# Column halves for the last output tile, and joined stores in the last chunk, of an attention and gated feed-forward kernel

## The chip, the cores and the metric

The kernel runs on one core of a Trainium2 chip. Its time is the device time of one execution in microseconds (us). The engines are called as the profile calls them: PE does the matmuls (PEld its weight loads), DVE, ACT and POOL do elementwise work, SP only issues transfers. Transfers run on 16 DMA engines; SP and ACT both issue them here, each into a queue of its own.

## What is computed

```python
# attention: q, k, v are (8, 8, 576, 64)
q_d = q.reshape(B, H, Sd, 4, D).mean(axis=3)          # and k_d, v_d
out_d = softmax(scale * q_d @ k_d.T) @ v_d
out_up = np.repeat(out_d, 4, axis=2)
mask = np.abs(pos[:, None] - pos[None, :]) < 4
out_local = softmax(where(mask, scale * q @ k.T, -1e9)) @ v
x = (out_up + out_local).transpose(0, 2, 1, 3).reshape(4608, 512)
# feed-forward
h = x @ w_in                                           # 512 -> 2048
g = h * np.clip(h + 3.0, 0.0, 6.0) / 6.0
out = g @ w_out                                        # 2048 -> 512, float32
```

The output is 4608 rows of 512 floats, so a row has 2048 bytes.

## The kernel before

The 4608 tokens are worked in nine chunks of 512. For each chunk the attention result is split into a high and a low part, multiplied by w_in, gated, split again and multiplied by w_out; each product is three matmuls (high by high, high by low, low by high). The last two chunks are planned together by `plan_pair`, which forms their first product in another way; their second product is ordinary again, in `gemm2` (L1392).

Every piece of work is an `op` of the class `Plan`, with an engine (or a choice), a cost, what it waits for and what it frees. `emit` (L1765) plays the plan through by these numbers and so decides the order in which the instructions are written out, engine by engine. The waits between engines are set afterwards by the framework, on semaphores. For transfers there are eight semaphores, called DMAHW0 to DMAHW7, taken in turn: a transfer waits until the one eight before it, on the same semaphore, has landed.

In the last chunk, the sums of the four output tiles (128 tokens by 512 columns each, m = 0 to 3) grow in four PSUM banks, o0 to o3. The last two blocks of w_out (`together`, L1402) are done tile by tile: six matmuls of 512 columns for tile 0, then for tile 1, 2 and 3 (L1420 to L1422). So the tiles become final one after the other. `plan_store` (L992) takes each of them out of PSUM with the factor 1/6: tiles 0 and 2 on ACT (L1013), 1 and 3 on DVE (L1015). It then stores the tile.

A tile can't be stored in one plain transfer. The output in DRAM is laid out so that 36 consecutive tokens of a batch entry lie 32 rows apart, and the next 36 tokens begin one row further. `stores` (L977) cuts a tile where such a group ends and yields the pieces (first partition, rows, place in DRAM); `put` (L988) issues one transfer for a piece. In the last chunk the pieces of a tile are sorted by size and dealt out in turn to SP and to ACT (L1023 to L1026). SP and ACT each do what stands in their queue in order, so an ACT eviction stands behind the stores ahead of it.

Of the kernel before, what the change touches and what calls it, by code (L numbers as in the profile page):

```python
# [13 lines left out]
AF = mybir.ActivationFunctionType  # L14
ALU = mybir.AluOpType
# [3 lines left out]
DM, DFF = 512, 2048  # L19
# [37 lines left out]
def tile_local_down_attention_moe(ctx, tc, q_all, k_all, v_all, _qk_loc, _v_loc, w_in, w_out, ident_d, _mask_d, out):  # L57
# [916 lines left out]
    otile, st_o, gemms = {}, {}, []  # L974
    n0 = len(PART) - 2

    def stores(t, cnt):  # L977

        p = 0
        while p < cnt:  # L980
            b, s = divmod(t + p, S)
            c, r = divmod(s, RP)
            k = min(RP - r, cnt - p)
            bp, b2 = divmod(b, NB2)
            yield p, k, (bp * NI * P + r * 32 + b2 * NC + c) * DM
            p += k

    def put(eng, ob, p, k, first):  # L988
        eng.dma_start(
            bass.AP(tensor=out.tensor, offset=out.offset + first, ap=[[32 * DM, k], [1, DM]]), ob[p:p + k])  # L990

    def plan_store(n, m, ready, frees):  # L992

        at = PART[n][0] + m * P
        ok = "ob" if n < n0 else "ob7"

        def ev(eng):
            st_o[n, m] = ob = buf(ok, (n, m), [P, DM])
            if eng is nc.scalar:
                eng.activation(ob, otile[n, m], AF.Copy, scale=1.0 / 6.0)  # L1000
            else:
                eng.tensor_scalar(ob, otile[n, m], 1.0 / 6.0, None, op0=ALU.mult)

        def store():
            for piece in stores(at, P):
                put(nc.sync, st_o[n, m], *piece)

        if n == len(PART) - 1:

            def ev_last(eng):  # L1010
                st_o[n, m] = buf("obz", (n, m), [P, DM])
                if eng is nc.scalar:
                    eng.activation(st_o[n, m], otile[n, m], AF.Copy, scale=1.0 / 6.0)  # L1013
                else:
                    eng.tensor_scalar(st_o[n, m], otile[n, m], 1.0 / 6.0, None, op0=ALU.mult)  # L1015

            def store_half(mine, eng):
                for piece in mine:
                    put(eng, st_o[n, m], *piece)

            e = [op("ACT" if m % 2 == 0 else "DVE", (0.60, 0.69)[m % 2], partial(ev_last, nc.scalar if m % 2 == 0 else nc.vector), [ready],
                    take=[("obz", (n, m))], free=[frees])]
            every = sorted(stores(at, P), key=lambda x: -x[1])  # L1023
            for eng, on_, mine in (("SP", nc.sync, every[0::2]), ("ACT", nc.scalar, every[1::2])):
                op(eng, 0.5 * len(mine), partial(store_half, mine, on_), e, free=[("obz", (n, m))],
                   size=dma(sum(k for _, k, _ in mine), 2048), nd=len(mine))  # L1026
            return
        e = op(on("ob", 1.0), 0, ev, [ready], take=[(ok, (n, m))], free=[frees], dl=start_of(n + 1) + TF * LAG)
        op("SP", 2.0, store, [e], free=[(ok, (n, m))], size=dma(P, 2048), dl=start_of(n + 1) + 10, nd=len(list(stores(at, P))))

    second = {}
# [1 line left out]
    def plan_moe(n):  # L1033
# [89 lines left out]
            plan.free_after(("gh" + k0, ("gh", key)), ops_)  # L1123
            plan.free_after(("gl" + k0, ("gl", key)), ops_)
        for m in range(nm):
            plan_store(n, m, ops_[m], (f"o{m}", n))
        return [last1]


# [10 lines left out]
    def plan_pair(prev_last, keeps):  # L1140
# [233 lines left out]
        for c in range(2):  # L1374
            n = n0 + c
            for i, f in enumerate(order):
                key = n, f

                def hi(eng, key=key):
                    parts7["h", key] = buf("ghb", ("gh", key), [P, TOK])  # L1380
                    copy_on(eng, parts7["h", key], gz[key])

                def lo(eng, key=key):
                    parts7["l", key] = buf("glb", ("gl", key), [P, TOK])
                    eng.tensor_tensor(parts7["l", key], gz[key], parts7["h", key].bitcast(F32), op=ALU.subtract)

                hold = [units_[-2][5], units_[-1][5]] if c or i > 1 else []
                d = op(on("ghi", TOK), 0, hi, [gz_ready[key]] + hold, take=[("ghb", ("gh", key))], lock=True)
                e = op(on("gl", TOK), 0, lo, [d], take=[("glb", ("gl", key))], free=[place_of(ORDER7.index(f // 2), key)], lock=True)
                parts7["ready", key] = [d, e]  # L1390

            def gemm2(m, f, n=n, c=c):  # L1392
                if f == order[0]:
                    otile[n, m] = bank(f"oe{m}" if c == 0 else f"o{m}", n)
                ms = slice(m * P, (m + 1) * P)
                gh, gl = parts7["h", (n, f)], parts7["l", (n, f)]
                for i, (gt, wt) in enumerate(((gh, 0), (gh, 1), (gl, 0))):
                    nc.tensor.matmul(  # L1398
                        otile[n, m], gt[:, ms], wout[f][:, wt],
                        start=(f == order[0] and i == 0), stop=(f == order[-1] and i == 2))  # L1400

            together = order[-2:] if c else order[-1:]  # L1402
            for i, f in enumerate(order):
                dl = base + len(ORDER7) * UNIT7 + (NF * c + i) * UNIT7 * 2 / 7
                after = parts7["ready", (n, f)] + [w_done["o", f]] + back.get(f, [])
                if f in together:
                    continue
                if i == 0:
                    ops_ = []
                    for m in range(4):  # L1410
                        ops_.append(op("PE", 0.683, partial(gemm2, m, f), after + prev[-1:], take=[(f"oe{m}" if c == 0 else f"o{m}", n)], dl=dl, rec=3))
                        prev.append(ops_[-1])
                else:
                    ops_ = [op("PE", 2.73, lambda f=f, g=gemm2: [g(m, f) for m in range(4)], after + prev[-1:], dl=dl, rec=12)]
                    prev += ops_
                for k in ("gh", "gl"):
                    plan.free_after((k + "b", (k, (n, f))), ops_)
            ops_ = []
            after = [x for f in together for x in parts7["ready", (n, f)] + [w_done["o", f]] + back.get(f, [])]
            for m in range(4):  # L1420
                ops_.append(op("PE", 0.683 * len(together), lambda m=m, g=gemm2, fs=together: [g(m, f) for f in fs], after + prev[-1:], dl=dl, rec=3 * len(together)))
                prev.append(ops_[-1])  # L1422
            for f in together:
                for k in ("gh", "gl"):
                    plan.free_after((k + "b", (k, (n, f))), ops_)
            for m in range(4):
                plan_store(n, m, ops_[m], (f"oe{m}" if c == 0 else f"o{m}", n))


    def busy(n):  # L1430
# [613 lines left out]
```

## Time and profile before

| | us |
|---|---|
| median of 3 runs (907.33 to 909.1) | 908.95 |
| the profiled execution, its own time | 907.05 |
| its span, first to last instruction | 905.3 |
| PE busy in the span | 885.7 (98%) |
| DVE, ACT, POOL busy | 631.4, 406.7, 224.8 |

The span is what the trace shows. The profiled execution took 1.75 us more than its span, and lies 1.9 us under the median of the timed runs.

### The profile page before, as it was taken

What the parts mean: (1) busy time and instruction counts of PE and PEld (TensorE: products, weight loads), DVE (VectorE), ACT (ScalarE), POOL (GpSimd) and SP (SyncE); (2) the same over time, 40 slices, a digit from 0 to 9 for tenths busy, and PEclk for the clock granted to TensorE, in tenths of its full rate; (3) what the DMA queues carried; (4) which work ended last, traced back from release to release, by engine and by line L of the source; (5) the groups of instructions that cost most, each with busy time, mean ns of one, the idle gap of its engine ahead of it and who ended that gap; (6) DMA issues with size and microseconds to landing.
All of it is one profiled execution on the core that took longest, in us unless ns stands there. A gap on an engine that the chain in (4) does not pass through costs nothing.

```text
span 905.3 us, 19616 instructions
## 1 busy us (share of the span) xinstructions
PE 885.7 (98%) x7044; PEld 720.5 (80%) x7044; DVE 631.4 (70%) x1174; ACT 406.7 (45%) x1404; POOL 224.8 (25%) x293
## 2 busy tenths in 40 slices
PE   8889999999999999999999999999999999999997
PEld 5667877887888888888888778888787888888886
DVE  6888987677836778676765785767666799964330
ACT  5786844656414446443432444335544344332100
POOL 2735554241301121211111210114222133400000
PEclk9999999999999999999999999999999999999999
DMA  9898667667624474754463656677665102222011
GB/s 217 222 272 272 168 145 133 131 126 141 131 71 89 95 148 99 144 101 97 99 137 72 120 113 164 151 183 185 170 140 117 23 24 70 76 88 104 31 29 47
DMA packets 325809, 111.94 MB, mean 124 GB/s; under 512 B 258640, under 2 KB 306640, under 8 KB 325712
## 3 DMA queue, kind: packets, MB, share of 16 engines
q1 hardware_dynamic: 325110, 109.92, 51.9%
q8 instruction: 56, 0.92, 0.4%
q10 hardware_dynamic: 602, 0.77, 0.3%
q14 instruction: 41, 0.34, 0.1%
HBM read 79.58 MB, written 31.05 MB: 122 GB/s over the span
## 4 chain that ended last, share of the span: by engine, by line
PE 84%; DMA 5%; SPq 5%; DVE 3%; issue 1%; ACT 1%; POOL 0%; DVEq 0%
PE o L1100 30%; PE h L1050 29%; PE o L1398 5%; PE o L1283 4%; PE h L1398 2%; PE a L1283 2%; PE a L1398 2%; SPq L373 2%; PE h L1283 2%; PE a L718 2%; PE h L761 1%; DMA arena<-in_v_dram 1%; DMA rows<-in_q_dram 1%; DMA early<-in_v_dram 1%; PE a L523 1%
## 5 line engine op out<-in xcount | busy, mean ns | idle before, releaser
L1050 PE MATMUL h<-rounded,wp 128*128 128x512 f32 x1344 | 318.3, 393 | 7.3 <-DVE arena L1060 5.0
L1100 PE MATMUL o<-wp,rounded 128*128 128x512 f32 x1344 | 323.1, 393 | 0.1
L1050 PEld LDWEIGHTS h<-rounded,wp 128*128 128x128 f32 x1344 | 252.1, 189 | 63.9 <-DVE arena L1060 7.2
L1100 PEld LDWEIGHTS o<-wp,rounded 128*128 128x128 f32 x1344 | 249.7, 188 | 53.5 <-DVE wp L211 0.5
L1056 ACT ACTIVATE arena<-h 128x512 f32<-128x512 f32 x112 | 66.3, 592 | 125.2 <-PE h L1050 116.1
L1060 DVE SCALAR_TENSOR_TENSOR arena<-arena,h 128x512 f32<-128x512 f32 x112 | 75.8, 677 | 50.9 <-ACT arena L1056 50.1
L573 ACT ACTIVATE arena<-arena 128x64 f32<-128x64 f32 x240 | 80.1, 336 | 0.5
L1068 DVE TENSOR_TENSOR rounded<-arena,rounded 128x512 fp32r<-128x512 f32 x83 | 58.8, 709 | 28.0 <-PE o L1100 24.8
L121 DVE CAST rounded<-arena 128x512 fp32r<-128x512 f32 (+1 forms) x93 | 43.0, 466 | 33.9 <-PE o L1100 17.4
L1068 POOL TENSOR_TENSOR rounded<-arena,rounded 128x512 fp32r<-128x512 f32 x29 | 39.4, 1358 | 97.4 <-PE o L1100 51.8
L379 DVE STREAM_TRANSPOSE arena<-arena 128x576 f32<-128x576 f32 x56 | 43.2, 774 | 28.2 <-DMA arena<-in_k_dram 14.2
L119 ACT CAST rounded<-arena 128x512 fp32r<-128x512 f32 (+6 forms) x57 | 36.9, 653 | 48.4 <-DVE arena L1060 19.8
L590 POOL TENSOR_TENSOR arena<-arena 128x640 f32<-128x640 f32 (+1 forms) x24 | 28.3, 1177 | 106.0 <-DVE arena L583 73.5
L454 POOL TENSOR_TENSOR arena<-arena 96x256 f32<-96x256 f32 (+1 forms) x23 | 18.4, 802 | 144.5 <-DMA arena<-in_v_dram 106.9
L452 DVE TENSOR_REDUCE arena<-arena 128x128 f32<-128x512 f32 (+1 forms) x31 | 33.2, 1075 | 19.8 <-DMA arena<-in_v_dram 10.3
L573 ACT ACTIVATION_READ_ACCUMULATOR arena<-arena 128x1 f32 x240 | 45.4, 189 | 0.0
L1398 PE MATMUL o<-wp,rounded 128*128 128x512 f32 x192 | 43.7, 389 | 0.0
L693 ACT ACTIVATE arena<-h 128x144 f32<-128x144 f32 x24 | 7.0, 290 | 79.1 <-PE h L677 79.1
L1398 PEld LDWEIGHTS o<-wp,rounded 128*128 128x128 f32 x192 | 36.1, 188 | 7.5
L549 ACT ACTIVATE arena<-arena 128x1 f32<-128x1 f32 (+1 forms) x78 | 15.1, 194 | 49.7 <-DVE arena L562 49.6
L411 DVE TENSOR_REDUCE arena<-arena 128x144 f32<-128x576 f32 x45 | 33.1, 742 | 1.9 <-PE h L523 1.6
L455 POOL TENSOR_TENSOR arena<-arena 96x128 f32<-96x128 f32 (+1 forms) x23 | 10.9, 474 | 88.7 <-PE h L677 81.1
(258 smaller groups left out, 1227.7 us busy)
## 6 DMA issues: line engine op xcount, KB each, us to landing
arena<-in_v_dram SPq DMA_DIRECT2D x58, 160.0 KB
pl<-arena SPq DMA_DIRECT2D x26, 320.0 KB
arena<-pl SPq DMA_DIRECT2D x104, 80.0 KB
rawp<-in_w_in_dram SPq DMA_DIRECT2D x16, 512.0 KB
rawp<-in_w_out_dram SPq DMA_DIRECT2D x16, 512.0 KB
arena<-in_q_dram SPq DMA_DIRECT2D x112, 72.0 KB
arena<-in_k_dram SPq DMA_DIRECT2D x112, 72.0 KB
arena<-in_v_dram SPq DMA_DIRECT2D x28, 256.0 KB
```

The lines of the kernel that those rows point to most:

```text
L119: nc.scalar.copy(out_, in_)
L121: eng.tensor_copy(out_, in_)
L379: nc.vector.transpose(out=qk[kind], in_=qk[kind])
L452: eng.tensor_reduce(out=vd, in_=raw.rearrange("p r e -> p e r"), op=ALU.add, axis=AX.X)
L573: nc.scalar.activation(x[:, j], x[:, j], AF.Exp, bias=m[:, j:j + 1], scale=0.125, accum_out=s[:, j:j + 1])
L1050: nc.tensor.matmul(st["ps"], win[f][:, wt, kk * P:(kk + 1) * P], xs[part][:, kk], start=(kk == 0 and i == 0), stop=(kk == NK - 1 and i == ...
L1056: nc.scalar.activation(st["t"], st["ps"], AF.Relu, bias=3.0)
L1060: nc.vector.scalar_tensor_tensor(out=t, in0=t, scalar=6.0, in1=st["ps"], op0=ALU.min, op1=ALU.mult)
L1068: eng.tensor_tensor(st["gl"], st["t"], st["gh"].bitcast(F32), op=ALU.subtract)
L1100: nc.tensor.matmul(otile[n, m], gt[:, ms], wout[f][:, wt], start=(f == 0 and i == 0), stop=(f == NF - 1 and i == 2),)
L1283: nc.tensor.matmul(ps[which], stationary(w, wt, kb), xs[x, kb][:, part], start=first and kb == 0 and q == 0, stop=last and kb == 1 and q = ...
L1398: nc.tensor.matmul(otile[n, m], gt[:, ms], wout[f][:, wt], start=(f == order[0] and i == 0), stop=(f == order[-1] and i == 2))
```

## The change

Three things are changed, all for the last chunk alone.

First, the six matmuls of the last tile (m = 3) become twelve of 256 columns: six for the left half, then six for the right half, in the same bank. Second, each half of that tile is taken out and stored on its own: the left half on DVE, the right half on ACT. Third, `stores` joins whole groups of 36 rows that follow one another, and `put` writes them as one transfer with three dimensions: groups, rows of a group, columns.

```diff
-    def stores(t, cnt):
+    def stores(t, cnt, joined=False):
         ...
             k = min(RP - r, cnt - p)
+            while joined and r == 0 and k % RP == 0 and k + RP <= min(cnt - p, S - s):
+                k += RP
         ...
-    def put(eng, ob, p, k, first):
+    def put(eng, ob, p, k, first, cs=slice(0, DM)):
+        width = cs.stop - cs.start
+        to = [[32 * DM, k]] if k <= RP else [[DM, k // RP], [32 * DM, RP]]
         eng.dma_start(
-            bass.AP(tensor=out.tensor, offset=out.offset + first, ap=[[32 * DM, k], [1, DM]]), ob[p:p + k])
+            bass.AP(tensor=out.tensor, offset=out.offset + first + cs.start, ap=to + [[1, width]]), ob[p:p + k, cs])
         ...
-            every = sorted(stores(at, P), key=lambda x: -x[1])
-            for eng, on_, mine in (("SP", nc.sync, every[0::2]), ("ACT", nc.scalar, every[1::2])):
-                op(eng, 0.5 * len(mine), partial(store_half, mine, on_), e, free=[("obz", (n, m))],
-                   size=dma(sum(k for _, k, _ in mine), 2048), nd=len(mine))
+            every = sorted(stores(at, P, True), key=lambda x: -x[1])
+            for h in range(halves):
+                cs = slice(h * DM // halves, (h + 1) * DM // halves)
+                name, eng = on_[(m + h) % 2]
+                e = op(name, (0.60, 0.69)[(m + h) % 2] / halves + 0.04 * (halves - 1), partial(ev_last, eng, cs), ready[h:h + 1] if halves > 1 else ready,
+                       take=[("obz", (n, m))], free=[frees])
+                for name, eng, mine in (("SP", nc.sync, every[0::2]), ("ACT", nc.scalar, every[1::2])):
+                    if mine:
+                        op(name, 0.5 * len(mine), partial(store_half, mine, eng, cs), [e], free=[("obz", (n, m))],
+                           size=dma(sum(k for _, k, _ in mine), 2048 // halves), nd=len(mine))
         ...
                 for i, (gt, wt) in enumerate(((gh, 0), (gh, 1), (gl, 0))):
                     nc.tensor.matmul(
-                        otile[n, m], gt[:, ms], wout[f][:, wt],
-                        start=(f == order[0] and i == 0), stop=(f == order[-1] and i == 2))
+                        otile[n, m][:, cs], gt[:, ms], wout[f][:, wt, cs],
+                        start=(f == order[0] and i == 0), stop=(f == order[-1] and i == 2 and cs.stop == DM), skip_group_check=True)
         ...
             for m in range(4):
-                ops_.append(op("PE", 0.683 * len(together), lambda m=m, g=gemm2, fs=together: [g(m, f) for f in fs], after + prev[-1:], dl=dl, rec=3 * len(together)))
-                prev.append(ops_[-1])
+                halves = 2 if c and m == 3 else 1
+                for h in range(halves):
+                    ops_.append(op(
+                        "PE", 0.683 * len(together) / halves,
+                        lambda m=m, g=gemm2, fs=together, cs=slice(h * DM // halves, (h + 1) * DM // halves): [g(m, f, cs=cs) for f in fs],
+                        after + prev[-1:], dl=dl, rec=3 * len(together)))
+                    prev.append(ops_[-1])
```

Outside of the last chunk the instructions of all five engines stand as before. PE's last matmuls before the change, with o3 the bank of the last tile, the weight blocks wp28 and wp29, and the split gated input in `rounded`:

```order
L1398 MATMUL o1_9203<-wp28_1491,rounded_66 128x512 x3
L1398 MATMUL o1_9203<-wp29_1571,rounded_66 128x512 x3
L1398 MATMUL o2_9211<-wp28_1491,rounded_66 128x512 x3
L1398 MATMUL o2_9211<-wp29_1571,rounded_66 128x512 x3
L1398 MATMUL o3_9215<-wp28_1491,rounded_66 128x512 x3
L1398 MATMUL o3_9215<-wp29_1571,rounded_66 128x512 x3
```

The same place with the change:

```order
L1410 MATMUL o2_9211<-wp28_1491,rounded_66 128x512 x3
L1410 MATMUL o2_9211<-wp29_1571,rounded_66 128x512 x3
L1410 MATMUL o3_9215<-wp28_1491,rounded_66 128x256 x3
L1410 MATMUL o3_9215<-wp29_1571,rounded_66 128x256 x3
L1410 MATMUL o3_9215<-wp28_1491,rounded_66 128x256 x3
L1410 MATMUL o3_9215<-wp29_1571,rounded_66 128x256 x3
```

Six matmuls of the last tile have become twelve narrower ones; nothing else of PE is moved.

SP's last ten transfers before the change, stores of the last chunk (rows by columns; the semaphores in brackets are those it waits for, DMAHW for an earlier transfer, ACT's or DVE's for the eviction):

```order
L989 DMA out_0_dram<-arena_65 36x512 [waits DMAHW4_49,Activation_49]
L989 DMA out_0_dram<-arena_65 36x512 [waits DMAHW5_49]
L989 DMA out_0_dram<-arena_65 8x512 [waits DMAHW7_49]
L989 DMA out_0_dram<-arena_65 36x512 [waits DMAHW1_49,DVE_49]
L989 DMA out_0_dram<-arena_65 32x512 [waits DMAHW3_49]
L989 DMA out_0_dram<-arena_65 36x512 [waits DMAHW5_49,Activation_49]
L989 DMA out_0_dram<-arena_65 36x512 [waits DMAHW6_49]
L989 DMA out_0_dram<-arena_65 4x512 [waits DMAHW0_49]
L989 DMA out_0_dram<-arena_65 36x512 [waits DMAHW2_49,DVE_49]
L989 DMA out_0_dram<-arena_65 36x512 [waits DMAHW4_49]
```

SP's last eight with the change:

```order
L993 DMA out_0_dram<-arena_65 3x36x512 [waits DMAHW4_49,Activation_49]
L993 DMA out_0_dram<-arena_65 8x512 [waits DMAHW5_49]
L993 DMA out_0_dram<-arena_65 2x36x512 [waits DMAHW7_49,DVE_49]
L993 DMA out_0_dram<-arena_65 24x512 [waits DMAHW0_49]
L993 DMA out_0_dram<-arena_65 3x36x512 [waits DMAHW2_49,Activation_49]
L993 DMA out_0_dram<-arena_65 4x512 [waits DMAHW4_49]
L993 DMA out_0_dram<-arena_65 3x36x256 [waits DMAHW6_49,DVE_49]
L993 DMA out_0_dram<-arena_65 3x36x256 [waits DMAHW7_49,Activation_49]
```

All joined transfers stand on SP's queue: one each for tiles 0, 1 and 2, and two for the halves of tile 3.

ACT's last instructions before the change, two evictions and eight stores:

```order
L1013 ACTIVATE arena_65<-o0_9197 128x512 [waits PE_49,Pool_49]
L989 DMA out_0_dram<-arena_65 36x512 [waits DMAHW3_49,Activation_49]
L989 DMA out_0_dram<-arena_65 12x512 [waits DMAHW6_49]
L989 DMA out_0_dram<-arena_65 36x512 [waits DMAHW0_49,DVE_49]
L989 DMA out_0_dram<-arena_65 24x512 [waits DMAHW2_49]
L1013 ACTIVATE arena_65<-o2_9211 128x512 [waits PE_49]
L989 DMA out_0_dram<-arena_65 36x512 [waits DMAHW4_49,Activation_49]
L989 DMA out_0_dram<-arena_65 16x512 [waits DMAHW7_49]
L989 DMA out_0_dram<-arena_65 36x512 [waits DMAHW1_49,DVE_49]
L989 DMA out_0_dram<-arena_65 20x512 [waits DMAHW3_49]
```

The same place with the change:

```order
L1021 ACTIVATE arena_65<-o0_9197 128x512 [waits PE_49,Pool_49]
L993 DMA out_0_dram<-arena_65 12x512 [waits DMAHW3_49,Activation_49]
L993 DMA out_0_dram<-arena_65 32x512 [waits DMAHW6_49,DVE_49]
L1021 ACTIVATE arena_65<-o2_9211 128x512 [waits PE_49]
L993 DMA out_0_dram<-arena_65 16x512 [waits DMAHW1_49,Activation_49]
L993 DMA out_0_dram<-arena_65 20x256 [waits DMAHW3_49,DVE_49]
L1021 ACTIVATE arena_65<-o3_9215 128x256 [waits PE_49]
L993 DMA out_0_dram<-arena_65 20x256 [waits DMAHW5_49,Activation_49]
```

ACT has a third eviction, the right half of tile 3, and five stores in place of eight, none of them joined. On DVE the eviction of tile 3 stays where it was, with 256 columns in place of 512. In the built program, this eviction and ACT's third one wait for the same count of PE's semaphore, the one that PE's very last matmul completes.

## Rows read from the trace of the kernel before

**Rows 1.** The page: busy time of each engine, and the head of the chain that ended last.

```profile
span 905.3 us, 19616 instructions
PE 885.7 (98%) x7044; PEld 720.5 (80%) x7044; DVE 631.4 (70%) x1174; ACT 406.7 (45%) x1404; POOL 224.8 (25%) x293
...
PE 84%; DMA 5%; SPq 5%; DVE 3%; issue 1%; ACT 1%; POOL 0%; DVEq 0%
```

**Rows 2.** The timeline of the tail, from several narrow stretches put in order: start, duration, engine, line, operation. SPq and ACTq are transfers being issued; the number after x is how many were merged into a row.

```profile
896.72 0.60 ACT L1013 ACTIVATE arena<-o 128x512 f32<-128x512 f32 x1 [37.06 <-PE o L1398]
897.34 0.30 SPq L989 DMA_DIRECT2D out_dram<-arena  x1
898.02 0.69 DVE L1015 TENSOR_SCALAR arena<-o 128x512 f32<-128x512 f32 x1 [12.91 <-PE o L1398]
898.80 0.31 SPq L989 DMA_DIRECT2D out_dram<-arena  x1
899.54 0.60 ACT L1013 ACTIVATE arena<-o 128x512 f32<-128x512 f32 x1 [2.22 <-DMA out_dram<-arena]
900.16 0.33 ACTq L989 DMA_DIRECT2D out_dram<-arena  x1
900.31 0.39 PE L1398 MATMUL o<-wp,rounded 128*128 128x512 f32 x1
900.74 0.69 DVE L1015 TENSOR_SCALAR arena<-o 128x512 f32<-128x512 f32 x1 [2.03 <-PE o L1398]
901.46 0.31 ACTq L989 DMA_DIRECT2D out_dram<-arena  x1
901.59 0.30 SPq L989 DMA_DIRECT2D out_dram<-arena  x1
902.34 0.30 SPq L989 DMA_DIRECT2D out_dram<-arena  x1
```

**Rows 3.** Busy time by stretches of the tail. The last two columns are the mean busy share of the 16 DMA engines and the GB/s that they moved.

```profile
897.30:898.10 0.80, 0.80 (x5) 0.64 (x5) 0.08 (x1) 0.01 (x1) 0.00 (x0) 1.00 0.00 0
898.10:898.20 0.10, 0.10 (x2) 0.10 (x1) 0.10 (x1) 0.00 (x0) 0.00 (x0) 1.00 0.72 184
...
898.25:898.50 0.25, 0.25 (x3) 0.19 (x1) 0.25 (x1) 0.00 (x0) 0.00 (x0) 1.00 0.73 188
898.50:898.75 0.25, 0.25 (x3) 0.21 (x2) 0.21 (x1) 0.00 (x0) 0.00 (x0) 1.00 0.75 197
...
901.00:901.25 0.25, 0.00 (x0) 0.00 (x0) 0.25 (x1) 0.00 (x0) 0.00 (x0) 1.00 0.73 180
901.25:901.50 0.25, 0.00 (x0) 0.00 (x0) 0.18 (x1) 0.00 (x0) 0.00 (x0) 1.00 0.73 172
...
903.75:904.00 0.25, 0.00 (x0) 0.00 (x0) 0.00 (x0) 0.00 (x0) 0.00 (x0) 1.00 0.03 8
904.00:905.30 1.30, 0.00 (x0) 0.00 (x0) 0.00 (x0) 0.00 (x0) 0.00 (x0) 0.91 0.00 0
```

**Rows 4.** DMA packets of four stretches, in turn: the whole tail (897.0 to 905.3), its last packets (903.69 to 903.92), the very last packet, a signal (903.87 to 903.90), and a stretch of loads and of a copy with 128 rows (640.1 to 640.9). A queue's row has packets, MB, and the time that they took as a share of 16 engines over the stretch; q1 is SP's, q10 ACT's. Packets under 512 B are in the tail those of 4 bytes that signal completion.

```profile
DMA packets 723, 1.06 MB, mean 127 GB/s; under 512 B 210, under 2 KB 210, under 8 KB 722
q1 hardware_dynamic: 408, 0.61, 23.2%
q10 hardware_dynamic: 314, 0.44, 18.7%
...
DMA packets 6, 0.01 MB, mean 27 GB/s; under 512 B 3, under 2 KB 3, under 8 KB 6
q1 hardware_dynamic: 6, 0.01, 7.6%
...
DMA packets 1, 0.00 MB, mean 0 GB/s; under 512 B 1, under 2 KB 1, under 8 KB 1
q1 hardware_dynamic: 1, 0.00, 1.9%
...
DMA packets 683, 0.21 MB, mean 257 GB/s; under 512 B 363, under 2 KB 683, under 8 KB 683
q1 hardware_dynamic: 683, 0.21, 103.0%
```

**Rows 5.** Issue times by line: least, median and most ns of one. L989 is the output stores (all of the span, then those of the tail), L612 and L620 are transfers with three dimensions, of 64 and of 32 partitions.

```profile
L989 SPq DMA_DIRECT2D out_dram<-arena x152: 252/364/1559, 154.9 to 902.3; - x152
L989 SPq DMA_DIRECT2D out_dram<-arena x10: 252/302/368, 897.3 to 902.3; - x10
L989 ACTq DMA_DIRECT2D out_dram<-arena x8: 307/340/643, 897.3 to 901.8; - x8
L612 SPq DMA_DIRECT2D pd<-arena x52: 580/609/639, 94.0 to 691.3; - x52
L620 SPq DMA_DIRECT2D arena<-pd x104: 303/462/1800, 98.5 to 695.1; - x104
```

**Rows 6.** The last piece of the chain on PE (start, us, what), and PE's weight loads of that stretch (busy us, mean ns of one).

```profile
857.18 43.53 PE o L1398 x192
...
L1398 PEld LDWEIGHTS o<-wp,rounded 128*128 128x128 f32 x191 | 35.9, 188 | 7.4
```

**Rows 7.** Instructions by shape, for narrow evictions: busy us, mean ns of one.

```profile
L693 ACT ACTIVATE arena<-h 128x144 f32<-128x144 f32 x24 | 7.0, 290 | 79.1 <-PE h L677 79.1
L459 DVE TENSOR_SCALAR arena<-arena,head 96x64 f32<-96x64 f32 x16 | 3.8, 276 | 0.3
L1239 DVE TENSOR_TENSOR arena<-arena 128x256 f32<-128x256 f32 x18 | 6.9, 417 | 0.5 <-POOL arena L1239 0.5
```

More of the change, by code (lines that the diff above doesn't have):

```diff
@@ L1008, in plan_store, with ev_last @@
         if n == len(PART) - 1:
-            def ev_last(eng):
-                st_o[n, m] = buf("obz", (n, m), [P, DM])
+            halves = 2 if m == 3 else 1
+            on_, last_ = (("ACT", nc.scalar), ("DVE", nc.vector)), []
+            def ev_last(eng, cs):
+                if (n, m) not in st_o:
+                    st_o[n, m] = buf("obz", (n, m), [P, DM])
                 if eng is nc.scalar:
-                    eng.activation(st_o[n, m], otile[n, m], AF.Copy, scale=1.0 / 6.0)
+                    eng.activation(st_o[n, m][:, cs], otile[n, m][:, cs], AF.Copy, scale=1.0 / 6.0)
@@ L1014, in ev_last, with store_half @@
                 else:
-                    eng.tensor_scalar(st_o[n, m], otile[n, m], 1.0 / 6.0, None, op0=ALU.mult)
-            def store_half(mine, eng):
+                    eng.tensor_scalar(st_o[n, m][:, cs], otile[n, m][:, cs], 1.0 / 6.0, None, op0=ALU.mult)
+            def store_half(mine, eng, cs):
                 for piece in mine:
-                    put(eng, st_o[n, m], *piece)
-            e = [op("ACT" if m % 2 == 0 else "DVE", (0.60, 0.69)[m % 2], partial(ev_last, nc.scalar if m % 2 == 0 else nc.vector), [ready],
-                    take=[("obz", (n, m))], free=[frees])]
@@ L1023, in plan_store @@
-            every = sorted(stores(at, P), key=lambda x: -x[1])
-            for eng, on_, mine in (("SP", nc.sync, every[0::2]), ("ACT", nc.scalar, every[1::2])):
-                op(eng, 0.5 * len(mine), partial(store_half, mine, on_), e, free=[("obz", (n, m))],
-                   size=dma(sum(k for _, k, _ in mine), 2048), nd=len(mine))
+                    put(eng, st_o[n, m], *piece, cs)
+            every = sorted(stores(at, P, True), key=lambda x: -x[1])
[8 more added lines that the diff above has]
+                           size=dma(sum(k for _, k, _ in mine), 2048 // halves), nd=len(mine))
@@ L1027, in plan_store @@
             return
-        e = op(on("ob", 1.0), 0, ev, [ready], take=[(ok, (n, m))], free=[frees], dl=start_of(n + 1) + TF * LAG)
+        e = op(on("ob", 1.0), 0, ev, ready, take=[(ok, (n, m))], free=[frees], dl=start_of(n + 1) + TF * LAG)
         op("SP", 2.0, store, [e], free=[(ok, (n, m))], size=dma(P, 2048), dl=start_of(n + 1) + 10, nd=len(list(stores(at, P))))
@@ L1125, in plan_moe @@
         for m in range(nm):
-            plan_store(n, m, ops_[m], (f"o{m}", n))
+            plan_store(n, m, [ops_[m]], (f"o{m}", n))
         return [last1]
@@ L1390, in plan_pair, with gemm2 @@
                 parts7["ready", key] = [d, e]
-            def gemm2(m, f, n=n, c=c):
-                if f == order[0]:
+            def gemm2(m, f, n=n, c=c, cs=slice(0, DM)):
+                if f == order[0] and cs.start == 0:
                     otile[n, m] = bank(f"oe{m}" if c == 0 else f"o{m}", n)
@@ L1426, in plan_pair @@
             for m in range(4):
-                plan_store(n, m, ops_[m], (f"oe{m}" if c == 0 else f"o{m}", n))
+                plan_store(n, m, ops_[m:m + 1 + c * (m == 3)], (f"oe{m}" if c == 0 else f"o{m}", n))
     def busy(n):
```

## The prediction

> **What bounds the kernel now.** The page comes first: PE is busy 98% of the span, and 84% of the chain that ended last is PE's [rows 1]. The change leaves all that as it is. Until the first store of the last chunk at 897.34, the instructions of the five engines stand as before. What can move is the tail, from there to the end of the span at 905.3.
>
> The timeline of the tail shows how it ends [rows 2]. PE's last matmul ends at 900.70 (900.31 plus 0.39). DVE takes tile 3 out until 901.43, and its four stores are issued at 901.46 and 901.81 on ACT, 901.59 and 902.34 on SP. The last one is late for its own reason: it waits for semaphore DMAHW4, that of the store which ACT issued at 900.16. So a 36-row store takes some 2.2 us until its semaphore is full. The windows show the rest [rows 3]: data begin 0.76 to 0.86 us after the first issue, and nothing starts after 904.00. The last packet of all begins after 903.87 [rows 4], and the span ends 1.4 us later, with signals, waits and closing steps. A store that ends later moves this whole end with it, one for one.
>
> The windows show a second thing, on which all hangs. While 36-row stores are under way, the DMA share stands at 0.72 to 0.75 [rows 3], though more stores wait. Transfers of 128 rows, in another stretch, fill all 16 engines (103%, since a packet counts where it starts) [rows 4]. 0.75 is 12 of 16, and 12 is the largest number up to 16 that divides 36. So a transfer is not dealt out packet by packet; its leading count is cut evenly over as many engines as divide it.
>
> **The change, part by part.** *PE.* Six matmuls become twelve of half the width. One of 512 takes 227 ns in the stream (43.53 us by 192), and a weight load 188 ns, now hidden beside it [rows 6]. The trace has no 256-column matmul with 128 by 128 weights of this kind. Twelve at half of 227 ns end when the six do now; twelve at 188 ns, if the weight load then sets the pace, end 0.9 us later (2.26 for 1.36). I take the 0.9, since that busy time is measured.
>
> *Evictions.* One of 0.69 us on DVE becomes two of 256 columns, on DVE and ACT. Both wait for PE's very last matmul, so the left half is not early; they run beside each other. For DVE the nearest rows are 276 ns (64 columns) and 417 ns (256 columns, two inputs), for ACT 290 ns at 144 columns and 597 at 512, which gives 380 on the line between [rows 2, 7]. By 0.42 in place of 0.69 the data are ready 0.27 us earlier.
>
> *Issuing.* SP issues 8 stores for 10, ACT 5 for 8, at some 0.3 us each now [rows 5]. The five joined ones have three dimensions. Such issues took from 0.30 us (L620) to 0.64 (L612) [rows 5]; the store's 108 partitions are nearer to L612's 64 than to L620's 32, so I take 0.6, and let the data start 0.3 later. ACT's freed issue time is worth nothing: its eviction of tile 2 began at 899.54 [rows 2], when that tile's matmuls had just ended (900.70 less six at 227 ns is 899.34).
>
> *The joined stores.* On the SBUF side such a store has 108 (or 72) partitions as its leading count, in DRAM 3 (or 2) groups. No transfer of the trace has sides that differ, so its spread must be bounded. The best end: the 108 rows count, 12 engines take 9 packets each, as three 36-row stores do now. The worst: one cut must serve both sides, only 3 (or 2) divides both, and each of 3 (or 2) engines carries 36 packets in a row. I take the worst: the only cut that the rows show is an even division of the leading count, and of the store's two leading counts 12 divides only one.
>
> The price follows from the packets. The last three rows and three signals of the tail take 7.6% of 16 engines over 0.23 us, 0.280 us; the signal alone takes 9 ns (1.9% of 16 over 0.03) [rows 4]. So a full row takes 84 ns; a half row, with a fixed part of 9 ns, (84 - 9) / 2 + 9 = 46 ns (bounds: 42, half a row, and 84, a whole one). A full row averages 104 ns over the tail, where both queues compete: (23.2 + 18.7)% of 16 over 8.26 us is 55.4, less 210 signals, by 512 rows [rows 4]. With 3 engines alone at work I take 84.
>
> If the 3 (or 2) engines are the same each time, the busiest carries 36 packets of each joined store: 108 full rows (9.07 us) and 72 half rows (3.31). To it come one or two packets of each of the other stores: eight full rows and four half ones (0.86). That is 13.24 us without a gap. It starts at 898.1 plus the 0.3, so it ends at 911.6, and with 1.4 us behind the last packet the span ends at 913.0. Nothing ahead comes too late for this: tile 1's joined store can start at 899.9, tile 2's at 901.3, and each finds the engine busy. SP's queue does not open a gap either. The 4-row store of tile 2 waits on DMAHW4 until tile 0's joined store has landed (near 902: 898.4, 36 packets, and a part of the 1.4 us), and both halves of tile 3 are queued behind it. The right half then waits on DMAHW7 for tile 1's, after 904.9 by such a part. Even with all of the 1.4 us its data could start at 907.2, and the engine is busy until 909.8 with what it has. PE's 0.9 us and the eviction's 0.27 vanish in that queue.
>
> So the span grows from 905.3 to 913.0, 7.8 us. The profiled execution, 907.05, would become 914.8; on the median, 908.95, it makes **916.7 us**.
>
> [...]
>
> **The rivals.** *Spread (not slower).* The 108 rows are dealt out as 36 are now. Then the path is PE, eviction, SP's two issues: PE ends at 900.70 to 901.60, the halves are out at 901.16 to 902.06, the left half is issued at 901.2, the right one at 901.8, and its data start at 902.9 and end, 9 packets later, near 903.3. With 1.4 us the span ends at 904.7, 0.6 sooner; with PE's 0.9 us it is 905.6, 0.3 later. So 908.3 to 909.3. For it speaks that both sides of the transfer have 108 rows in the same order, against it that the rows show a cut only in the leading count. How many engines are enough: the joined stores hold 288 full and 216 half rows, 34.1 us of one engine; with n engines the span ends at 898.4 + 34.1 / n + 0.86 + 1.4, which is under 907.1 (1.8 more than now) from n = 6 on.
>
> *Confined, but each store to engines of its own.* Then the stores run beside each other, and only the last counts. The right half waits until tile 1's joined store has landed: issue 898.8, data at 899.9, 36 rows until 902.9, landed near 903.3 (0.4 of the 1.4 us; the rows don't divide it). It is then issued at 903.4, starts at 904.5, takes 36 by 46 ns until 906.2, and the span ends at 907.6: 2.3 us more, 911.3. The trace's rows don't name engines, so nothing there excludes it; but the share of 0.75 held while several stores of 36 were under way on two queues, which speaks for the same 12 each time.
>
> *The split of tile 3 is the bound.* Should twelve matmuls cost more than 0.9 us, it shows only in the spread case, where each 1 us of PE is 1 us.
>
> **How the numbers follow.** Confined to the same engines: 0.68. Confined to changing ones: 0.09. Spread: 0.23. The first alone reaches from 914.3 (the base of the profiled execution, no later start, 42 ns for a half row) to about 920 (104 ns for a full row, 57 for a half one). To leave out no more than 2 in 10, the range takes in the changing engines and most of the spread case: 908.4 to 920. About 0.2%, 1.8 us, is what a measurement of this kernel can tell from no change. The first case is slower by 0.86%, the second by 0.25%, so slower has 0.68 and nearly all of the 0.09; the spread case is within 0.2%, but for a small chance that it gains more. That makes 0.76 slower, 0.22 the same, 0.02 faster.
>
> **What would show it.** The DMA share of the tail falls from 0.75 to about 0.19 (3 of 16) and, towards the end, 0.13, with some 50 to 75 GB/s. PE still ends near 901. The last issue on SP stands near 905, held by DMAHW7, and the data run on to about 911.6. It is wrong if the share in the tail stays at 0.7, or if the last SP issue stands at 902; it is wrong in its price if a full row on a lone engine takes far from 84 ns.

## The result, and the profile after

The changed kernel takes 917.24 us (median of 6 runs, 915.03 to 919.76) against 908.75 for the kernel before in the same series. The two medians are 8.5 us apart (0.93%); the ratio on record, formed over the runs and not from the two medians, is 1.0109, 95% interval 1.0088 to 1.0130. The prediction was 916.7 us, with 0.76 for slower. Its profiled execution took 915.03, with a span of 913.2 (before: 907.05 and 905.3 [rows 1]).

The page of the changed kernel shows that the engines' work is as before, within 1.5 us on each.

```profile
span 913.2 us, 19626 instructions
PE 884.2 (97%) x7050; PEld 719.9 (79%) x7050; DVE 630.0 (69%) x1174; ACT 407.4 (45%) x1405; POOL 225.7 (25%) x293
...
PE 84%; DMA 5%; SPq 4%; DVE 4%; issue 1%; ACT 1%; ACTq 0%; DVEq 0%
```

The timeline of its tail, from several stretches put in order (start, duration, engine, line, operation; the number after x counts merged issues, whose duration is from the first to the last):

```profile
893.72 4.99 PE L1410 MATMUL o<-wp,rounded 128*128 128x512 f32 x27
895.28 11.73 SPq L993 DMA_DIRECT2D out_dram<-arena  x8
895.96 0.69 DVE L1023 TENSOR_SCALAR arena<-o 128x512 f32<-128x512 f32 x1 [12.91 <-PE o L1410]
898.75 0.42 DVE L1023 TENSOR_SCALAR arena<-o 128x256 f32<-128x256 f32 x1 [2.10 <-PE o L1410]
899.30 0.33 ACTq L993 DMA_DIRECT2D out_dram<-arena  x1
899.67 0.38 ACT L1021 ACTIVATE arena<-o 128x256 f32<-128x256 f32 x1 [1.76 <-DVE arena L1023]
902.01 0.73 SPq L993 DMA_DIRECT2D out_dram<-arena  x1
902.01 5.00 SPq L993 DMA_DIRECT2D out_dram<-arena  x2
```

PE ends at 898.71 (893.72 plus 4.99). Before, the span ended 4.6 us behind PE's last matmul (900.70 to 905.3 [rows 2, 3]); now it ends 14.5 us behind it. I call this stretch, from PE's end to the end of the span, the tail's length; it is free of what differs from run to run ahead of it. The last two rows show SP's last two issues: the left half's at 902.01, for 0.73, and the right half's, which ends at 907.01. SP stood still between them, and the waits on SP in that stretch say for what (engine, line, waited for: us, times, longest):

```profile
SPq L993 <- DMA out_dram<-arena: 3.5, 1, 3.5
```

Busy time by stretches of the tail; as in [rows 3], the last two columns are the mean share of the 16 DMA engines and their GB/s:

```profile
896.25:896.50 0.25, 0.25 (x3) 0.21 (x2) 0.25 (x1) 0.00 (x0) 0.00 (x0) 1.00 0.12 33
896.50:896.75 0.25, 0.25 (x3) 0.21 (x2) 0.15 (x1) 0.00 (x0) 0.00 (x0) 1.00 0.00 0
896.75:897.00 0.25, 0.25 (x3) 0.21 (x2) 0.00 (x0) 0.00 (x0) 0.00 (x0) 1.00 0.18 57
...
898.00:899.00 1.00, 0.71 (x6) 0.51 (x5) 0.25 (x1) 0.00 (x0) 0.00 (x0) 1.00 0.45 68
...
902.00:903.00 1.00, 0.00 (x0) 0.00 (x0) 0.00 (x0) 0.00 (x0) 0.00 (x0) 1.00 0.30 42
...
904.00:905.00 1.00, 0.00 (x0) 0.00 (x0) 0.00 (x0) 0.00 (x0) 0.00 (x0) 0.50 0.19 68
...
906.00:907.00 1.00, 0.00 (x0) 0.00 (x0) 0.00 (x0) 0.00 (x0) 0.00 (x0) 0.50 0.20 77
...
909.00:910.00 1.00, 0.00 (x0) 0.00 (x0) 0.00 (x0) 0.00 (x0) 0.00 (x0) 0.50 0.20 72
910.00:911.00 1.00, 0.00 (x0) 0.00 (x0) 0.00 (x0) 0.00 (x0) 0.00 (x0) 0.50 0.12 43
911.00:912.00 1.00, 0.00 (x0) 0.00 (x0) 0.00 (x0) 0.00 (x0) 0.00 (x0) 0.50 0.07 25
912.00:912.25 0.25, 0.00 (x0) 0.00 (x0) 0.00 (x0) 0.00 (x0) 0.00 (x0) 0.50 0.01 4
912.25:913.20 0.95, 0.00 (x0) 0.00 (x0) 0.00 (x0) 0.00 (x0) 0.00 (x0) 0.50 0.00 0
```

Where [rows 3] had 0.72 to 0.75 and 172 to 197 GB/s, the share now stands at 0.19 to 0.20, which is 3 of 16 (0.19), with 68 to 77 GB/s, for six microseconds in which no compute engine works. Before that the share is higher in two of the rows above (0.45 and 0.30) but the rate is not (68 and 42 GB/s): packets took longer there (from 898 to 899 ten packets of ACT's queue took 26.9% of 16 engines, 430 ns each on the mean), and the share counts a packet's whole time. The joined data begin at 896.77 and end at 912.08.

### The profile page after: what moved, and what is told of

It reads as the page before. It is cut to its first block, busy times and chain, and to the rows that moved or that the text cites. A ratio compares the mean times of both kernels' runs of the same rounds, so it can differ in the third digit from the quotient of the medians.

```text
span 913.2 us, 19626 instructions
## 1 busy us (share of the span) xinstructions
PE 884.2 (97%) x7050; PEld 719.9 (79%) x7050; DVE 630.0 (69%) x1174; ACT 407.4 (45%) x1405; POOL 225.7 (25%) x293
## 4 chain that ended last, share of the span: by engine, by line
PE 84%; DMA 5%; SPq 4%; DVE 4%; issue 1%; ACT 1%; ACTq 0%; DVEq 0%
PE o L1112 30%; PE h L1062 30%; PE o L1410 5%; PE o L1295 4%; PE a L1410 2%; PE h L1410 2%; PE a L1295 2%; PE h L1295 2%; PE a L718 2%; PE h L761 1%; SPq L373 1%; DMA arena<-in_k_dram 1%; PE a L523 1%; DMA early<-in_v_dram 1%; DMA rows<-in_q_dram 1%
## 5 line engine op out<-in xcount | busy, mean ns | idle before, releaser
L1112 PE MATMUL o<-wp,rounded 128*128 128x512 f32 x1344 | 322.8, 393 | 0.0
L452 DVE TENSOR_REDUCE arena<-arena 128x128 f32<-128x512 f32 (+1 forms) x31 | 33.2, 1077 | 20.8 <-DMA arena<-in_v_dram 12.2
L1410 PE MATMUL o<-wp,rounded 128*128 128x512 f32 (+1 forms) x198 | 43.8, 383 | 0.0
```

The source lines that it names most:

```text
L452: eng.tensor_reduce(out=vd, in_=raw.rearrange("p r e -> p e r"), op=ALU.add, axis=AX.X)
L1112: nc.tensor.matmul(otile[n, m], gt[:, ms], wout[f][:, wt], start=(f == 0 and i == 0), stop=(f == NF - 1 and i == 2),)
L1410: nc.tensor.matmul(otile[n, m][:, cs], gt[:, ms], wout[f][:, wt, cs], start=(f == order[0] and i == 0), stop=(f == order[-1] and i == 2 an ...
```

## The experiments

Each theory had to say which part of the change costs, and why. The ratios are those on record against the kernel before on the same chip, its median 907.8 to 908.6; they are not quotients of the medians. A tail's length is read from one profile of each run.

**Which part: the halves, or the joined stores?** First the changed kernel with only the halves kept:

```diff
-            every = sorted(stores(at, P, True), key=lambda x: -x[1])
+            every = sorted(stores(at, P), key=lambda x: -x[1])
```

> The change without joining: the last tile is still computed, taken out and stored by column halves, but each group of 36 rows goes out in a store of its own. Measure: from the end of PE's last matmul to the end of the span, 4.6 us before the change and 14.5 us with it. Theory (joined stores are confined to 3 or 2 engines): 4.3 to 5.3 us, DMA share in the tail at 0.6 to 0.75, time within 0.2% of before. Rival (the halves are what costs: 1 KB rows, the twelve matmuls, the evictions one behind the other): most of the 9.9 us stays, 12 us or more.

Measured: ratio 0.9989 (0.9964 to 1.0014), 906.16 us. The tail is 4.9 us long (PE's last matmul ends at 904.59, the span at 909.5), 0.3 more than before, and the DMA share stays at 0.58 to 0.65 from 902.5 to 906.5. Two rows of its timeline show what became of the halves:

```profile
904.63 0.42 DVE L1023 TENSOR_SCALAR arena<-o 128x256 f32<-128x256 f32 x1 [2.10 <-PE o L1410]
906.05 0.38 ACT L1021 ACTIVATE arena<-o 128x256 f32<-128x256 f32 x1 [2.09 <-DMA out_dram<-arena]
```

The right half, on ACT, is taken out 1.4 us behind the left one, though both were ready at once: ACT first issued the stores that stand ahead of it in its order, and stood idle for 2.09 us until a transfer had landed. So cutting the tile costs no measurable time here, and brings none.

Then only the joined stores, with tile 3 whole:

```diff
-            halves = 2 if m == 3 else 1
+            halves = 1
...
-                halves = 2 if c and m == 3 else 1
+                halves = 1
...
```

> The joining without the halves: tile 3 is computed, taken out and stored whole, but its three full groups go out in one store. Theory (confined to the same 3 or 2 engines): the busiest engine has 144 full rows in place of 108 full and 72 half ones, 0.3 us less by 84 and 46 ns; from PE's end to the end of the span 13.5 to 15.5 us, DMA share about 0.19 and then less, time about 1.0% above before. Rival (the halves cost): 4.6 us, as before.

Measured: ratio 1.0100 (1.0062 to 1.0138), 916.94 us; tail 14.6 us, as in the full change (14.5). Two of its windows:

```profile
909.00:911.00 2.00, 0.00 (x0) 0.00 (x0) 0.00 (x0) 0.00 (x0) 0.00 (x0) 0.50 0.20 77
911.00:913.00 2.00, 0.00 (x0) 0.00 (x0) 0.00 (x0) 0.00 (x0) 0.00 (x0) 0.50 0.20 77
```

With the halves alone within noise of before, the joining is the cost.

**Why: the spread over engines, or something else in a joined store?** The same five joined stores with the two outer dimensions of the DRAM side exchanged, so that it leads with 36 instead of 3 (or 2):

```diff
-        to = [[32 * DM, k]] if k <= RP else [[DM, k // RP], [32 * DM, RP]]
+        to = [[32 * DM, k]] if k <= RP else [[32 * DM, RP], [DM, k // RP]]
```

> The whole change, but the two outer dimensions of a joined store are exchanged in DRAM: 36 rows of a group first, groups inside. Each of the five joined stores has the same rows, bytes and queue; the output rows inside these groups land in another order. Theory (the number of engines is the largest up to 16 that divides both leading counts): 108 and 36 give 12 engines, the DMA share of the tail is back at 0.6 to 0.75, and from PE's end to the end of the span it takes 4.2 to 5.5 us; the time is within 0.2% of before. Rival (a store of 108 rows or of three dimensions, or few large stores, is slow as such): 12 us or more, as in the change.

Measured: ratio 1.0006 (0.9983 to 1.0030), 908.16 us. A row of its timeline and one of its windows:

```profile
895.50 6.18 SPq L993 DMA_DIRECT2D out_dram<-arena  x8
```

```profile
897.20:898.20 1.00, 1.00 (x10) 0.96 (x9) 0.00 (x0) 0.60 (x1) 0.00 (x0) 1.00 0.78 248
```

The same bytes, rows, three dimensions and eight issues: the share reaches 0.78 (plain stores stand beside the joined ones in this stretch), SP is done at 901.68 instead of 907.01, and the tail is 5.3 us long (PE ends at 898.9) instead of 14.5. The order of two numbers in the DRAM side's description is what the change costs. With it the rows land in another order, which this run alone doesn't part from the count of engines; in the cuts below the rows move too, and there the leading count parts long tails from shorter ones.

Then the other way round: the kernel before, where nothing is joined and nothing halved, with the 36 rows of each of the last chunk's eleven 36-row stores described as 3 by 12:

```diff
-            bass.AP(tensor=out.tensor, offset=out.offset + first, ap=[[32 * DM, k], [1, DM]]), ob[p:p + k])
+            bass.AP(tensor=out.tensor, offset=out.offset + first, ap=([[32 * DM, 3], [3 * 32 * DM, RP // 3]]
+                    if cut and k == RP else [[32 * DM, k]]) + [[1, DM]]), ob[p:p + k])
...
-                    put(eng, st_o[n, m], *piece)
+                    put(eng, st_o[n, m], *piece, True)
```

> The kernel before, without joining and without halves; only each 36-row store of the last chunk has its DRAM side written as 3 by 12 rows, so that its leading count is 3 (the output rows inside a group land in another order). Theory (confined): eleven stores of 12 packets on each of the same 3 engines, 132 full rows on the busiest and some 8 more, 11.8 us at 84 ns and up to 14 if a row takes 100: from PE's end to the end of the span 11 to 14 us. Rival (joining as such is slow): 4.6 to 5.5 us, since no store is joined; the three dimensions alone cost some 0.3 us of issue time for each.

Measured: ratio 1.0091 (1.0060 to 1.0121), 914.93 us; tail 12.2 us. Two rows of its windows:

```profile
900.20:901.20 1.00, 0.00 (x0) 0.00 (x0) 0.00 (x0) 0.00 (x0) 0.00 (x0) 0.81 0.20 78
901.20:902.20 1.00, 0.00 (x0) 0.00 (x0) 0.00 (x0) 0.00 (x0) 0.00 (x0) 0.50 0.20 76
```

Stores of two queues were under way in this stretch (over the two microseconds SP's queue took 9.4% of the 16 engines and ACT's 10.8%), and still only 3 engines' worth of work is seen: the leading 3 does it without any joining, and the stores of both queues share the same 3 engines.

**How the cost grows with the leading count.** The same cut with 6 and with 12 in place of 3:

> As the run with each 36-row store cut 3 by 12 (12.2 us from PE's end to the end of the span), but cut 6 by 6. Theory (engines as the leading count divides): 66 packets on the busiest of 6 engines, 5.5 us at 84 ns, so the engines stop being the limit; SP's seven issues of some 0.73 us and three of 0.3 are then about as long (6.0 us from its first issue, 3.4 before PE's end), and 5.3 to 6.5 us are expected. Rival (three dimensions, or another order of the rows, are slow as such): 10 us or more.

> The same, cut 12 by 3: 12 engines, as many as a plain 36-row store has, with the same three dimensions and number of stores. Theory: the engines cost what they cost before (4.6 us from PE's end to the end of the span), and only the longer issues on SP show: 5.0 to 6.2 us, no more than in the cut by 6. Rival (three dimensions as such): 10 us or more.

Measured for 6: 1.0049 (1.0024 to 1.0075), 911.44 us, tail 8.4 us. For 12: 1.0015 (0.9993 to 1.0038), 911.51 us, tail 7.3 us. In the tails the order 3, 6, 12 is as the theory has it, 12.2, 8.4 and 7.3 us, though 6 and 12 have medians that are alike, some 3 us above the kernel before, so the times don't part them. In the cut by 6 the DMA share from 907.0 to 908.0, behind the last issue, was 0.37, near the 0.38 of 6 engines in 16. The rows land in another order in all three, so another order as such is not what makes the cut by 3 slow. Both tails are longer than expected. A row of SP's timeline of each says why, 6 first:

```profile
898.20 8.46 SPq L989 DMA_DIRECT2D out_dram<-arena  x10
```

```profile
901.51 8.02 SPq L989 DMA_DIRECT2D out_dram<-arena  x10
```

Ten issues take SP 8.5 and 8.0 us, against 5.3 before (897.34 to 902.34 plus 0.30 [rows 2]): the cut stores have three dimensions, and SP's issues took 0.74 and 0.77 us at the median and 0.88 and 0.91 at most, against 0.30 and 0.37 [rows 5]. In the cut by 12, whose share went up to 0.69 (907.2 to 908.2), the span ends 2.7 us behind SP's last issue, as it does before (902.64 to 905.3), which points to SP's issuing as the bound there, and no longer the engines. The two runs therefore don't give a clean price per engine.

**One joined store alone.** Only tile 3's rows joined, and the tile whole (`halves = 1`, as above), all else as before:

```diff
-            every = sorted(stores(at, P, True), key=lambda x: -x[1])
+            every = sorted(stores(at, P, m == 3), key=lambda x: -x[1])
```

> The kernel before, with a single joined store: the three full groups of tile 3, stored whole. Measure: from the end of PE's last matmul to the end of the span (4.6 us before, 14.5 with the change). Theory (confined, the price goes by packets): eviction until 0.7, issue at 0.9, data 1.4 after that, 36 full rows at 84 ns on each of 3 engines (3.0), then 1.3 to the end: 6.0 to 7.0 us. Rival (a joined store has a fixed cost, or only several in a row hurt): 4.6 to 5.3 us, or more than 8.

Measured: ratio 1.0054 (1.0035 to 1.0073), 912.42 us; tail 8.4 us, 1.4 more than the upper end expected, and in the range that was given to the rival (a fixed cost). Its 36 packets per engine should have taken 3.0 us; the data ran from 900.7 to 905.5, 4.8 us. The packets of that stretch in two parts, 900.6 to 902.7 and 902.7 to 905.9:

```profile
DMA packets 32, 0.06 MB, mean 29 GB/s; under 512 B 2, under 2 KB 2, under 8 KB 32
q1 hardware_dynamic: 30, 0.06, 16.9%
...
DMA packets 81, 0.16 MB, mean 50 GB/s; under 512 B 3, under 2 KB 3, under 8 KB 81
q1 hardware_dynamic: 81, 0.16, 14.1%
```

In the first part 30 packets of q1 took 16.9% of 16 engines over 2.1 us, 5.7 us: 190 ns each on the mean, not 84. In the second part 78 rows took 93 ns each (14.1% of 16 engines over 3.2 us). So one joined store behind everything else lengthens the tail by 3.8 us, where five lengthen it by 9.9, and 1.8 of the 3.8 us are a surplus over 84 ns a row, all of it in the first 3 us (from 903.6 on a row took 84 ns).

**Why the rows were dearer than 84 ns.** The full change has such a surplus too (below). Is it the other stores on the same engines? The joined stores of the joined-only run again, without the others (the short pieces of the last chunk aren't stored):

```diff
-            every = sorted(stores(at, P, True), key=lambda x: -x[1])
+            every = [x for x in stores(at, P, True) if x[1] > RP]
```

> The joining without the halves, and all stores of the last chunk that are not joined left out (their output rows aren't written). It asks where the 2 us go by which the sum of 13.24 us was too short. Theory A (other stores share the engines and their queues, and hold the joined ones up): alone they run at 80 to 84 ns a row, 144 rows on the busiest engine are 11.5 to 12.1 us from the first data, and from PE's end to the end of the span it takes 11.0 to 12.2 us. Theory B (the joined stores are slow by themselves at first, while PE still runs, or a row costs more than 84 ns): 13 us or more.

Measured: 916.61 us, ratio 1.0079 (1.0054 to 1.0104), tail 13.2 us. SP's row in the timeline, then the packets of 899.5 to 905.5 and of 907.0 to 909.0:

```profile
898.05 4.82 SPq L993 DMA_DIRECT2D out_dram<-arena  x4
```

```profile
DMA packets 152, 0.31 MB, mean 52 GB/s; under 512 B 3, under 2 KB 3, under 8 KB 151
q1 hardware_dynamic: 151, 0.30, 18.9%
...
DMA packets 78, 0.15 MB, mean 77 GB/s; under 512 B 3, under 2 KB 3, under 8 KB 78
q1 hardware_dynamic: 78, 0.15, 19.8%
```

In the first six microseconds a row took 122 ns (18.9% of 16 engines over 6 us is 18.1, by 148 rows), later 84 (19.8% over 2 us is 6.34, by 75). The other stores are not the reason: the surplus is there without them. Nor are all rows dearer. By the trace's single packets, 119 of the 148 rows took 100 ns or less, as later, and 22 took 200 to 638 ns; one that began at 903.88 took 638. The rows stalled now and then, and between 902.0 and 903.5 hardly at all: 47 rows took 92 ns each (18.0% of 16 engines over 1.5 us).

The run settles a second matter. From 902.9 on all four stores were issued and none but these were there, and yet the share is 3 of 16 (0.19 on the mean from 903.0 to 905.0, and 0.19 to 0.20 in each microsecond from there to 910.0). Stores on engines of their own would have run beside each other, with a larger share. A queue that worked one store after the other would have shown tile 1's two engines (2 of 16, 0.13) in the middle. They show at the end:

```profile
909.00:910.00 1.00, 0.00 (x0) 0.00 (x0) 0.00 (x0) 0.00 (x0) 0.00 (x0) 0.50 0.19 76
911.00:912.00 1.00, 0.00 (x0) 0.00 (x0) 0.00 (x0) 0.00 (x0) 0.00 (x0) 0.50 0.13 51
912.00:913.00 1.00, 0.00 (x0) 0.00 (x0) 0.00 (x0) 0.00 (x0) 0.00 (x0) 0.50 0.13 51
```

The last 3 us are 36 rows of 84 ns on two engines. These two carry 144 rows each and the third 108, since tile 1's store is not on it. So the stores stand behind each other on the same three engines, and tile 1's on two of them.

Is it PE's work that slows the first rows? The same four stores with 48 more matmuls, which nobody reads, behind the last:

```diff
         plan.emit(warm, gemms[0], busy)
+        more = psum.tile([P, 512], F32, name="h1", tag="h1")
+        for _ in range(48):
+            nc.tensor.matmul(
+                more, identb, identb.unsqueeze(1).broadcast_to([P, 4, P]), start=True, stop=True,
+                skip_group_check=True)
```

> The four joined stores alone, as in the run without the other stores (the remaining stores of the last chunk are left out again), and behind the last real matmul PE goes on with 48 matmuls that nobody reads, some 10 us. In the run without them the first two joined stores landed 5.1 and 3.5 us apart from the data's start and from each other, the last two 2.9 us apart each, which is 36 rows at 80 ns. Theory A, the slow packets belong to PE's work and the few us behind it: with PE at work until some 912, all four are slow, 3.5 us or more apart, and the fourth lands 15 us or more after the data's start. Theory B, they belong to the first rows of the tail, or to some 6 us of it, whatever PE does: the last two land 2.9 us apart as before, the fourth some 14 us after the data's start. The span itself says little here, since PE is part of it.

Measured: 914.36 us in one run. PE's added work in the timeline, then the packets of 897.5 to 903.8 and of 904.0 to 908.0:

```profile
899.19 10.53 PE L1495 MATMUL h<-identb 128*128 128x512 bf16 x48
```

```profile
DMA packets 163, 0.33 MB, mean 53 GB/s; under 512 B 3, under 2 KB 3, under 8 KB 162
q1 hardware_dynamic: 162, 0.33, 19.2%
...
DMA packets 153, 0.31 MB, mean 77 GB/s; under 512 B 3, under 2 KB 3, under 8 KB 153
q1 hardware_dynamic: 153, 0.31, 19.7%
```

With PE at work until 909.7 the picture is the same: 122 ns a row for six microseconds, then 84. So the change to 84 ns does not wait for PE to fall idle. A last try, which meant to begin the four stores behind tile 3's eviction, says little more:

> The four joined stores alone again (the other stores of the last chunk are left out), but all four issued behind tile 3's eviction instead of each behind its own tile's. The data then begin some 2.3 us after PE's last matmul, not 1.9 us ahead of it. Theory A, the slow packets belong to the stretch that ends some 5 us after PE's last matmul: only the first store is slow, the other three land 2.9 us apart each, and the data run 12.1 to 13.0 us (144 rows at 84 ns are 12.1). Theory B, they belong to the first rows or the first 6 us of confined stores: the first two are slow again (near 5 and 3.5 us), and the data run 13.6 us or more.

Measured: 914.43 us in one run. Its first joined store was issued at 895.75, 3.4 us ahead of PE's end, exactly as without the edit, since the real waits follow the data and not the plan's order. It only repeats the run with the joined stores alone: the data ran 14.2 us, 13.8 there.

Taken together, the surplus over 84 ns a row was 1.8 us with one joined store (4.8 us for 3.0), 1.7 with four alone (13.8 for 12.1, with PE at work too), 2.1 in the last try and 2.1 in the full change (below). It did not grow with the number of stores, so it looks like a cost once per tail and not like a price per row. What causes it stays open. It needs no other stores, and it ended while PE still worked. It is no fixed time from the first joined store either: the last stall began 2.9 us after the first joined data in the run with one, 5.5 to 6.2 us after it in the runs with four. In all of these runs, the full change with them, it began 3.6 to 5.5 us behind PE's last real matmul, so that stretch of time, whatever PE does in it, stays a rival: stores that begin behind it were not run. The issuing on SP is a weaker one: with one store and with four the last stall began 2 to 3 us behind SP's last issue, but in the full change no row stalled behind the issue at 906.3.

## Why the prediction was right, and where its sum was not

**The spread.** The step on which all hung holds: the joined stores run on 3 engines (2 for tile 1's), the same each time. The exchange of two dimensions takes the cost away (ratio 1.0006, tail 5.3 us), and the leading 3 without any joining brings most of it (1.0091, tail 12.2 us). So "spread" is refuted by the share, and "confined to changing engines" by the end of the four stores alone. Measured were 3 of 16 for 108 against 3 (0.19 to 0.20), 2 of 16 for 72 against 2 (0.13, in the four stores alone), and up to 0.78 for 108 against 36. That one cut has to serve both leading counts was an estimate, read from the share of 0.72 to 0.75 for 36 rows [rows 3]; these three cases fit it, and for leading counts that were not run nothing here shows it. Which engines they are no trace here names.

**The sum.** The span came out as 913.2 for 913.0, and that is luck, for two deviations cancel. The part ahead of the tail happened to be 2.1 us shorter (first store issued at 895.28; 897.34 before), and the tail itself 2.2 us longer than the sum: 17.9 us from the first store's issue to the end of the span, 15.7 forecast. The sum of 7.8 us for the change is short in the same way: the tail behind PE's end grew by 9.9 us. The medians, 8.5 us apart, lie between; that 916.7 came so near to 917.24 owes something to the scatter of the runs. Point by point:

- *The packets' stretch*, forecast 13.24 us, measured 15.3 (896.77 to 912.08). This is the mis-sized term. The sum took 84 ns per row from the last rows of the tail, for the reason that 3 engines would work alone; the tail's own mean of 104 ns [rows 4] was put down to two queues competing. The stores alone refute this reason: with a single queue, the first 148 rows took 122 ns each on the mean. By the prediction's own sign (a full row far from 84 ns) its price was wrong there; what it left out is some 2 us at the start. The two later prices were right: 84 ns a full row, and 46 a half row, as the packets of 910.9 to 911.9 in the changed kernel show (6.6% of 16 engines over 1 us, by 23):

```profile
q1 hardware_dynamic: 23, 0.02, 6.6%
```

- *The start*, forecast 1.06 us behind the first joined issue, measured 1.49 (895.28 to 896.77; the data in the windows before 896.75 are those of ACT's 12-row store). Forecast was 0.6 us for an issue with three dimensions; the eight on SP took 722 ns in the median. The issues of the tail (line 993, least, median and most ns):

```profile
L993 SPq DMA_DIRECT2D out_dram<-arena x8: 264/722/1725, 895.3 to 906.3; - x8
L993 ACTq DMA_DIRECT2D out_dram<-arena x5: 298/329/1256, 895.3 to 901.8; - x5
```

- *Behind the last packet*, forecast 1.4, measured 1.1 (912.08 to 913.2). With the other two: 2.1 and 0.4 less 0.3 is the tail's 2.2.
- *PE.* Forecast 0.9 us for twelve narrow matmuls. From DVE's start on tile 1 to its start on tile 3 it is 2.79 us (895.96 to 898.75), 2.72 before (898.02 to 900.74 [rows 2]): they cost 0.07. The weight load of 188 ns was not the pace, and the other bound, nothing, was right. In this queue it made no difference, as forecast.
- *The evictions.* 0.42 us on DVE and 0.38 on ACT, as forecast, but not side by side: ACT began at 899.67, half a microsecond behind DVE's end, because the left half's 20-row store (issued at 899.30) stands ahead of it on ACT and waits for DVE. The error is one of order on ACT; in the halves-only run the two halves are 1.4 us apart for the same reason, and that run gained nothing.
- *SP's queue.* As forecast, the right half was held until tile 1's joined store had landed; its issue began near 906.3, 1.3 us later than said for the dearer rows, and opened no gap of weight: the share stays at 0.19 to 0.20 until 910. Earlier the share had not fallen to 0.19, as the prediction's sign had it: it was 0.45 and 0.30 in the rows of 898 and 902 above, and only the rate, 68 and 42 GB/s, lay in the range forecast or below it.

## What to carry to other kernels

Before joining transfers, look at the leading count on both sides of the new one. Here 108 against 3 gave a share of 0.19 to 0.20 and a tail of 14.5 us; with 36 in place of 3 the share reached 0.78 and the tail was 5.3 us, with the same eight issues on SP. The two issues fewer than before were worth nothing when the transfer had three engines instead of twelve. The row of the profile that tells it is the DMA share of a stretch in which nothing else moves: 0.75 is 12 engines of 16, 0.19 is three. Read the GB/s beside it: while packets stalled in the changed kernel, the share was 0.30 and the rate 42 GB/s (902 to 903); later it was 0.20 with 77 GB/s (906 to 907). And take the price of a packet from the mean of such a stretch as well as from its end; where the two differ, the reason for the difference is a guess until it is tried.

## What was not expected of the hardware

- The first rows of confined stores took 122 ns on the mean for six microseconds in the runs with four, and 190 ns for two microseconds in the run with one, then 84. Most of these rows (half in the run with one) took no more than 100; some stalled for 200 to over 600 ns. This added about 2 us to a tail, with one store as with five. The cause is open, and whether it needs confined stores was not tried.
- The joined stores, with three dimensions, took SP 0.68 to 0.86 us to issue in the run with them alone, and plain issues behind confined stores took up to 1.73 us on SP and 1.26 on ACT (368 and 643 ns at most in the tail before, though up to 1559 on SP over the whole span [rows 5]). What such an issue waits for wasn't tried.
- Twelve matmuls of 256 columns, each with weights of 128 by 128, cost 0.07 us more than six of 512 (2.79 us against 2.72, from DVE's start on tile 1 to its start on tile 3).
